# Retention and MLP on one core: order of the first loads, w_in's second half in two transfers, the last product in two PSUM banks

## Chip, core and metric

The kernel runs on one core of a Trainium2 chip. Its time is the device time of one launch, in microseconds. The core's engines are called PE (matmul), DVE (vector), ACT (scalar), POOL (GpSimd) and SP (sync); each runs its own instructions in order, and they wait for one another through semaphores. SP and ACT issue DMAs whose descriptors are made in hardware (queues q1 and q10 of the profile). POOL issues DMAs whose descriptors it makes itself (q0), and these can change the data type on the way. All three kinds run on the same 16 DMA engines.

## What is computed

```python
# q, k, v: [8, 8, 576, 64] float32; moe_w_in: [512, 2048]; moe_w_out: [2048, 512]
scores = (1 / sqrt(64)) * q @ k.transpose(0, 1, 3, 2)
gamma  = 1 - 2.0 ** (-5 - arange(8))
Dmat   = where(i >= j, gamma[h] ** (i - j), 0)
attn   = (scores * Dmat) @ v                     # [8, 8, 576, 64]
x      = attn.transpose(0, 2, 1, 3).reshape(4608, 512)
h      = x @ moe_w_in
out    = maximum(0.01 * h, h) @ moe_w_out        # [4608, 512] float32
```

The first part is a retention: attention without a softmax, with a decay per head. The second is an MLP with a leaky ReLU.

## The kernel before

**Units and groups.** The 4608 tokens are cut into 36 units of 128 tokens, two chunks of 64 each. A unit's q, k and v are 256 KB each (128 partitions x 512 float32), loaded by `load(u)` into tiles `t32` in the order k, q, v (x = 1, 0, 2). Four units make a group of 512 tokens, for which the MLP runs with float16 weights.

**Retention of a unit.** `cast_k` (ACT), `cast_q` and `cast_v` (DVE for the first eight units, POOL later) make float16 tiles, the last two with a decay multiplied in. The casted q and k are transposed, by PE into PSUM and a copy for units 0 to 7 (`transpose_pe`, `transposed`, `turn`), by a DMA that SP issues for the others (`transpose_dma`). `scores(u)` multiplies k with q inside a chunk and k with v for the state. `masks(u)` applies the causal mask on DVE. `state(u, j)` adds up the state on DVE, `state_cast` casts it. `outputs` or `outputs_acc` make the unit's 128 columns of x, which go to `xT`. `ahead(u)` is casts and transpose of a unit by ACT, POOL and SP.

**MLP.** `h_block`, `h_half` and `h_unit` are products with w_in (PE, L373), each followed by a leaky ReLU on ACT (L387) that empties an accumulator `acc`, of which there are four, one PSUM bank each. `h_half(g, a, fb)` takes half a of the group's tokens and 256 columns of the hidden layer, so fb = 0, 1 lie in the first quarter of w_in, fb = 2, 3 in the second, 4, 5 in the third and 6, 7 in the fourth. `halves` is several of these in a row. Group 0's product with w_out is `wide` (L423). Those of the other groups are `seven` (L483): seven products of 16 matmuls each in place of eight, with sums of weights (`w_mix`) and of activations (`mix`, DVE) prepared, and `keep` and `give` to bring the products p1, p5, p6 and p7 together. `give` writes a part of the output tile `osb`, and SP stores it. In the last group the second token half is stored in pieces: `give(1, 1, ...)` stores one, and the very last `give(1, 0, ...)` is done in two parts of 128 tokens.

**Order.** The program's order is written out by hand (`manual_schedule`), so the calls' order is each engine's order. It opens with `keep_warm` matmuls on zeros, the loads of units 0 to 7 with the weights between them, and the retention of units 0 to 3. Then groups 0 and 1 of the MLP are woven with units 4 to 7, and from there on each group's MLP is woven with the retention of later units.

**Loads at the start.** SP issues unit 0's k, the first half of its q and unit 1's k. ACT issues identity, constants and the other half of unit 0's q. POOL issues all the rest, in this order: v of unit 0, q and v of unit 1, units 2 and 3, the first two quarters of w_in, unit 4, the third quarter, unit 5, the fourth quarter, units 6 and 7, w_out. A quarter of w_in is two DMAs (64 partitions, four rows of 512 columns each, cast from float32 to float16). Each DMA of POOL uses one of eight semaphores in turn, and waits for the landing of the one eight before it. `behind` makes a DMA wait for other DMAs. `load(8)`, which SP issues, waits in this way for the third of the w_out loads.

Of the kernel before, what the change touches and what calls it, by code (L numbers as in the profile page):

```python
# [9 lines left out]
FP = mybir.dt.float32  # L10
F16 = mybir.dt.float16
MUL = mybir.AluOpType.mult
ADD = mybir.AluOpType.add
# [5 lines left out]
def kernel(  # L19
# [9 lines left out]
    nc = tc.nc  # L29
# [3 lines left out]
    P = 128  # L33
# [8 lines left out]
    HF, HN, HT = NF // 2, DM // 2, TOK // 2  # L42
# [99 lines left out]

    FQ = DFF // 4

    def load_w_in(f, after=None):
        fs = slice(f * FQ, (f + 1) * FQ)
        rows = moe_w_in.rearrange("(o c k) f -> o k c f", o=2, k=CH)
        ds = []
        for o in range(2):
            ds.append(nc.gpsimd.dma_start(out=w_in16[half(o), :, fs], in_=rows[o][:, :, fs]))  # L150
            if after is not None and not o:
                behind(ds[0], *after)
        return ds
# [298 lines left out]
    def g_part(g, a, b):  # L452
        return g_t[g][:, b * HF : (b + 1) * HF, a * HT : (a + 1) * HT]
# [15 lines left out]
    def seven(g, hooks, last=False):  # L469
# [2 lines left out]
        s = sums[g]  # L472

        def product(name, lhs, rhs, fresh):
            if fresh:
                r[name] = acc_pool.tile([P, 2, HN], FP, name="acc")
            order = (
                [(f, tb) for tb in range(2) for f in range(HF)]
                if last
                else [(f, tb) for f in range(HF) for tb in range(2)]  # L480
            )
            for n, (f, tb) in enumerate(order):
                nc.tensor.matmul(  # L483
                    out=r[name][:, tb, :],
                    lhsT=lhs[:, f, tb * P : (tb + 1) * P],
                    rhs=rhs[:, f, :],
                    start=fresh and n == 0,
                    stop=f == HF - 1,
                    skip_group_check=True,
                )  # L490

        def keep(name, of, plus=None):
            r[name] = m_pool.tile([P, 2, HN], FP, name=name)
            if plus is None:
                nc.scalar.copy(out=r[name], in_=r[of])
            else:
                nc.vector.tensor_tensor(out=r[name], in0=r[of], in1=r[plus], op=ADD)

        def give(a, b, of, plus=None, parts=1):
            if ("o", a) not in r:  # L500
                r["o", a] = o_pool.tile([P, 2, DM], FP, name="osb")
            for n in range(parts):
                ts = slice(n * 2 // parts, (n + 1) * 2 // parts)
                to = r["o", a][:, ts, b * HN : (b + 1) * HN]
                if plus is None:
                    nc.scalar.copy(out=to, in_=r[of][:, ts])
                else:
                    nc.vector.tensor_tensor(  # L508
                        out=to, in0=r[of][:, ts], in1=r[plus][:, ts], op=ADD
                    )  # L510
# [16 lines left out]
            ("p5", s[:, 0], w_mix[:, 0], True, lambda: keep("v", "p5", "u2")),  # L527
            ("p7", g_part(g, 1, 0), w_mix[:, 2], True, lambda: give(1, 1, "p7", "v")),
            ("p5", g_part(g, 0, 0), w_part(1, 1), False, lambda: give(0, 1, "p5", "u2")),
            (  # L530
                "p7", g_part(g, 1, 1), w_mix[:, 3], False,
                lambda: give(1, 0, "p7", "u2", 2 if last else 1),
            ),
        )
        if last:
            plan = (plan[0], plan[2], plan[1]) + plan[3:]
# [21 lines left out]
    pool_copy, act_copy, dve_copy = nc.gpsimd.tensor_copy, nc.scalar.copy, nc.vector.tensor_copy  # L558

    keep_warm(7)  # L560
    load(0, {1: nc.sync, 0: (nc.sync, nc.scalar), 2: nc.gpsimd})
    load(1, {1: nc.sync, 0: nc.gpsimd, 2: nc.gpsimd})
    load(2, nc.gpsimd)
    load(3, nc.gpsimd)
    load_w_in(0)
    load_w_in(1)
    load(4, nc.gpsimd)
    load_w_in(2)
    load(5, nc.gpsimd)
    load_w_in(3)  # L570
    load(6, nc.gpsimd)
    load(7, nc.gpsimd)
    w_out_loads = [d for n in range(4) for d in load_w_out(n)]


# [10 lines left out]
    for u in range(4):  # L586
# [7 lines left out]
        if not u:  # L594
            cast_q(1, nc.vector)
            cast_v(1, nc.vector)
        state(u, 1)
        if n < 4:
            transpose_pe(n, 1)
# [9 lines left out]
        if n < 3:  # L609
            cast_k(n + 1)  # L610
            cast_q(n + 1, nc.vector)
            cast_v(n + 1, nc.vector)
        if u < 3:
            state_cast(u, act_copy, (1,))
        if u == 1:
# [8 lines left out]
    def halves(g, *items):  # L624
        for a, fb in items:
            h_half(g, a, fb)
# [64 lines left out]
    halves(0, (0, 0), (0, 1))  # L691
    finish2(3)
    state_cast(3, act_copy, (1,))
    halves(0, (0, 2), (0, 3), (1, 0))
    cast_k(4)
    cast_qv(4)
    halves(0, (1, 1))
    turn(4, 1)
    halves(0, (1, 2))
    turn(4, 0)  # L700
# [128 lines left out]
```

## Time and profile before

| | |
|---|---|
| median of 14 runs | 292.47 us (291.36 to 297.07) |
| profiled execution | 291.36 us |
| its span, first to last instruction | 289.6 us |
| instructions | 9449 |
| busy PE, DVE, ACT, POOL | 281.1, 170.2, 144.2, 104.6 us |
| granted PE clock | 0.998 |
| read from HBM, written to it | 36.81 MB, 9.44 MB |
| first product with w_in begins | 18.66 us |

A line of the profile names engine and program line, then what an instruction writes and reads: "PE L373 MATMUL acc<-xT,w_in" is a product of line 373. A bracket at its end gives the idle time before it and who ended it. PEld is the weight load of a matmul. Stretches are given in microseconds from the start of the span. A row of a DMA view gives KB of one transfer and the median time from issue to landing; a row of a queue gives packets, megabytes and share of the 16 engines' time in that window. Busy POOL time in the first 36 us is mostly the issuing of DMAs.

### The profile page before, as it was taken

Reading aid. Unit: us, or ns where it says so; the run is one execution under the profiler, and the core shown is the slowest. Engines: PE = TensorE matmul, PEld = TensorE weight load, DVE = VectorE, ACT = ScalarE, POOL = GpSimd, SP = SyncE. Lnnn points to the kernel's source line nnn. Section 1 sums busy time; section 2 is a strip of 40 time slices with the busy share of each in tenths; the row PEclk is TensorE's granted clock in tenths of the full one; section 3 lists DMA queues with packets and bytes.
Section 4 is the critical chain, followed back from the end, with each engine's and each line's share of the span. In section 5 each row is a group of like instructions: output and inputs, shape, how many; then the busy total and the mean of one; then the engine's idle time right before and its main releaser. Section 6 shows DMA issues by size and latency. Waiting matters only on the chain.

```text
span 289.6 us, 9449 instructions
## 1 busy us (share of the span) xinstructions
PE 281.1 (97%) x4118; PEld 191.9 (66%) x4118; DVE 170.2 (59%) x293; ACT 144.2 (50%) x254; POOL 104.6 (36%) x124
## 2 busy tenths in 40 slices
PE   6999999999999999999999999999999999999994
PEld 2568888745874587458745874587458844874583
DVE  1875677964763595359635863586268636841342
ACT  3666766624327732773277327731773176317510
POOL 8959502843433324322524332234225413000000
PEclk9999999999999999999999999999999999999999
DMA  7999999998999977966896669788976151012003
GB/s 207 301 234 198 295 207 216 210 231 188 255 201 285 224 167 165 273 147 149 165 268 153 147 147 284 153 145 150 278 162 145 44 177 38 5 67 80 0 2 145
DMA packets 131738, 50.01 MB, mean 173 GB/s; under 512 B 121264, under 2 KB 126000, under 8 KB 131696
## 3 DMA queue, kind: packets, MB, share of 16 engines
q1 hardware_dynamic: 124864, 39.46, 58.7%
q0 software_dynamic: 6016, 9.70, 14.8%
q8 instruction: 32, 0.52, 0.7%
q10 hardware_dynamic: 816, 0.24, 0.3%
q14 instruction: 10, 0.08, 0.1%
HBM read 36.81 MB, written 9.44 MB: 160 GB/s over the span
## 4 chain that ended last, share of the span: by engine, by line
PE 91%; DVE 4%; DMA 2%; issue 1%; ACT 1%; ACTq 0%; DVEq 0%
PE acc L373 43%; PE acc L483 34%; PE acc L423 5%; PE sc L215 3%; DMA t<-in_q_dram 2%; PE ot L291 1%; PE sc L224 1%; PE ot L302 1%; PE ot L321 1%; PE acc L200 1%; DVE s L233 1%; DVE qk L175 1%; DVE v L179 1%; PE ot L333 0%; PE acc L551 0%
## 5 line engine op out<-in xcount | busy, mean ns | idle before, releaser
L373 PE MATMUL acc<-xT,w_in 128*128 128x512 f16 (+2 forms) x768 | 130.9, 326 | 0.0
L387 ACT ACTIVATE gt<-acc 128x512 f16<-128x512 f32 x144 | 85.9, 597 | 57.1 <-PE acc L373 55.4
L373 PEld LDWEIGHTS <-w_in 128*128 128x128 f16 x768 | 68.1, 98 | 51.3
L483 PEld LDWEIGHTS <-gt 128*128 128x128 f16 x640 | 61.8, 98 | 9.1
L233 DVE TENSOR_TENSOR s<-sc,cs 128x512 f16<-128x512 f32 x36 | 24.7, 687 | 40.8 <-PE sc L224 40.8
L273 POOL CAST st<-s 128x512 f16<-128x512 f32 x21 | 12.8, 610 | 93.5 <-DVE s L257 57.9
L483 PE MATMUL acc<-w_out,gt 128*128 128x256 f16 x384 | 45.9, 273 | 0.2
L355 ACT COPY own<-ot 128x512 f32<-128x512 f32 x30 | 17.6, 586 | 42.7 <-PE ot L302 34.9
L175 POOL TENSOR_TENSOR qk<-t,cs 128x512 f16<-128x512 f32 x28 | 30.6, 1094 | 15.6 <-DMA t<-in_q_dram 14.4
L179 POOL TENSOR_TENSOR v<-t,cs 128x512 f16<-128x512 f32 x28 | 31.6, 1130 | 0.2 <-PE acc L373 0.2
L467 DVE TENSOR_TENSOR mix<-gt 128x1024 f16<-128x1024 f16 x16 | 14.7, 916 | 29.0 <-ACT gt L387 29.0
L483 PE MATMUL acc<-w_mix,gt 128*128 128x256 f16 x256 | 30.6, 273 | 0.0
L483 PE MATMUL acc<-w_mix,mix 128*128 128x256 f16 x256 | 29.5, 273 | 0.0
L483 PEld LDWEIGHTS <-mix 128*128 128x128 f16 x256 | 25.0, 98 | 3.1 <-DVE mix L467 0.2
L172 ACT CAST qk<-t 128x512 f16<-128x512 f32 x36 | 22.3, 620 | 0.8 <-DMA t<-in_k_dram 0.6
L360 DVE TENSOR_TENSOR xT<-ot,own 128x512 f16<-128x512 f32 x30 | 20.5, 683 | 3.0 <-ACT own L355 3.0
L257 DVE TENSOR_TENSOR s<-sc,s 128x256 f32<-128x256 f32 x40 | 16.8, 420 | 3.3 <-PE sc L224 2.8
L508 DVE TENSOR_TENSOR osb<-acc,u 128x512 f32<-128x512 f32 (+1 forms) x17 | 11.1, 656 | 8.0 <-PE acc L483 8.0
L215 PEld LDWEIGHTS <-qkT 64*64 64x64 f16 x576 | 7.7, 107 | 11.2 <-issue 10.1
L276 POOL CAST st<-s 128x256 f16<-128x256 f32 x7 | 3.2, 454 | 32.2 <-DVE s L261 20.3
L423 PE MATMUL acc<-w_out,gt 128*128 128x512 f16 x64 | 14.3, 379 | 0.0
L467 DVE TENSOR_TENSOR mix<-mix,gt 128x1024 f16<-128x1024 f16 x16 | 14.0, 879 | 0.5
(52 smaller groups left out, 239.3 us busy)
## 6 DMA issues: line engine op xcount, KB each, us to landing
out_dram<-osb SPq DMA_DIRECT2D x17, 512.0 KB, 3.8
t<-in_k_dram SPq DMA_DIRECT2D x27, 256.0 KB, 3.9
t<-in_q_dram SPq DMA_DIRECT2D x25, 256.0 KB, 4.5
t<-in_v_dram SPq DMA_DIRECT2D x25, 256.0 KB, 4.9
w_in<-in_moe_w_in_dram POOLq DMA_DIRECT2D x8, 256.0 KB, 7.1
w_out<-in_moe_w_out_dram POOLq DMA_DIRECT2D x4, 512.0 KB, 9.9
t<-in_v_dram POOLq DMA_DIRECT2D x7, 256.0 KB, 5.3
t<-in_q_dram POOLq DMA_DIRECT2D x6, 256.0 KB, 5.7
```

What stands on the lines that cost most here:

```text
L172: nc.scalar.copy(out=qk16[u][:, 1], in_=t32[u, 1])
L175: eng.tensor_tensor(out=qk16[u][:, 0], in0=t32[u, 0], in1=decay(u, 0), op=MUL)
L179: eng.tensor_tensor(out=v16[u], in0=t32[u, 2], in1=decay(u, 1), op=MUL)
L233: nc.vector.tensor_tensor(out=s16s[u], in0=sc_tiles[u][:, :, 0], in1=mask_sb.unsqueeze(1).unsqueeze(1).to_broadcast([P, 2, NP, CH]), op=MUL,)
L257: nc.vector.tensor_tensor(out=to, in0=st, in1=carry[0], op=ADD)
L355: nc.scalar.copy(out=owns[u], in_=ot_tiles[u][:, :, 0:NP].rearrange("q j c t -> q c j t"))
L360: nc.vector.tensor_tensor(out=x_of(u).rearrange("q (c g) t -> q c g t", g=2), in0=ot_tiles[u][:, :, NP : 2 * NP].rearrange("q g (c j) t -> ...
L373: nc.tensor.matmul(out=hps[:, n, :], lhsT=w_in16[:, c, f * P : (f + 1) * P], rhs=xT[g][:, c, ts], start=(c == 0), stop=(c == NP - 1),)
L387: nc.scalar.activation(out=out, in_=in_, func=mybir.ActivationFunctionType.Lrelu)
L423: nc.tensor.matmul(out=ys[tb], lhsT=g_t[0][:, f, tb * P : (tb + 1) * P], rhs=w_out16[:, f, :], start=(f == 0), stop=(f == NF - 1),)
L467: nc.vector.tensor_tensor(out=z[:, fs], in0=a[:, fs], in1=b[:, fs], op=op)
L483: nc.tensor.matmul(out=r[name][:, tb, :], lhsT=lhs[:, f, tb * P : (tb + 1) * P], rhs=rhs[:, f, :], start=fresh and n == 0, stop=f == HF - ...
```

## The change

- Unit 0's v is issued in two halves by SP and ACT, behind their halves of q, in place of POOL.
- POOL's first DMA is then unit 1's q, and it waits for unit 0's k to land.
- `cast_v` of units 2 and 3 moves from behind `cast_q` to behind the mask of the unit before.
- The third and fourth quarter of w_in are loaded together, in two DMAs with rows of 1024 columns; the loads of units 5, 6 and 7 follow.
- In group 0, `h_half` (1, 0) moves behind the casts of unit 4.
- Casts and transpose of unit 9 (`ahead(9)`) come in front of `load(11)`.
- In the last group, p7 uses an accumulator for each of its two token blocks, with both of its `give` calls in two parts and stores.

```diff
-    def load_w_in(f, after=None):
-        fs = slice(f * FQ, (f + 1) * FQ)
+    def load_w_in(f, n=1, after=None):
+        fs = slice(f * FQ, (f + n) * FQ)
...
         def product(name, lhs, rhs, fresh):
+            apart = last and name == "p7"
             if fresh:
-                r[name] = acc_pool.tile([P, 2, HN], FP, name="acc")
+                r[name] = [
+                    acc_pool.tile([P, 1 if apart else 2, HN], FP, name="acc")
+                    for _ in range(2 if apart else 1)
+                ]
...
-                    out=r[name][:, tb, :],
+                    out=r[name][tb][:, 0, :] if apart else r[name][0][:, tb, :],
...
-                    start=fresh and n == 0,
+                    start=fresh and (f == 0 if apart else n == 0),
...
-        def give(a, b, of, plus=None, parts=1):
+        def give(a, b, of, plus=None):
+            parts = len(r[of])
...
-            (
-                "p7", g_part(g, 1, 1), w_mix[:, 3], False,
-                lambda: give(1, 0, "p7", "u2", 2 if last else 1),
-            ),
+            ("p7", g_part(g, 1, 1), w_mix[:, 3], False, lambda: give(1, 0, "p7", "u2")),
...
-    load(0, {1: nc.sync, 0: (nc.sync, nc.scalar), 2: nc.gpsimd})
-    load(1, {1: nc.sync, 0: nc.gpsimd, 2: nc.gpsimd})
+    load(0, {1: nc.sync, 0: (nc.sync, nc.scalar), 2: (nc.sync, nc.scalar)})
+    load(1, {1: nc.sync, 0: nc.gpsimd, 2: nc.gpsimd}, {0: (last_load[0, 1],)})
     load(2, nc.gpsimd)
     load(3, nc.gpsimd)
     load_w_in(0)
     load_w_in(1)
     load(4, nc.gpsimd)
-    load_w_in(2)
-    load(5, nc.gpsimd)
-    load_w_in(3)
-    load(6, nc.gpsimd)
-    load(7, nc.gpsimd)
+    load_w_in(2, 2)
+    for u in range(5, 8):
+        load(u, nc.gpsimd)
...
         if not u:
             cast_q(1, nc.vector)
             cast_v(1, nc.vector)
+        elif n < 4:
+            cast_v(n, nc.vector)
         state(u, 1)
...
             cast_q(n + 1, nc.vector)
-            cast_v(n + 1, nc.vector)
...
-    halves(0, (0, 2), (0, 3), (1, 0))
+    halves(0, (0, 2), (0, 3))
     cast_k(4)
     cast_qv(4)
-    halves(0, (1, 1))
+    halves(0, (1, 0), (1, 1))
...
+    ahead(9)
     load(11)
-    ahead(9)
```

More of the change, by code (lines that the diff above doesn't have):

```diff
@@ L494, in keep @@
             if plus is None:
-                nc.scalar.copy(out=r[name], in_=r[of])
+                nc.scalar.copy(out=r[name], in_=r[of][0])
             else:
-                nc.vector.tensor_tensor(out=r[name], in0=r[of], in1=r[plus], op=ADD)
-        def give(a, b, of, plus=None, parts=1):
+                nc.vector.tensor_tensor(out=r[name], in0=r[of][0], in1=r[plus], op=ADD)
+        def give(a, b, of, plus=None):
+            parts = len(r[of])
             if ("o", a) not in r:
@@ L505, in give @@
                 if plus is None:
-                    nc.scalar.copy(out=to, in_=r[of][:, ts])
+                    nc.scalar.copy(out=to, in_=r[of][n])
                 else:
                     nc.vector.tensor_tensor(
-                        out=to, in0=r[of][:, ts], in1=r[plus][:, ts], op=ADD
+                        out=to, in0=r[of][n], in1=r[plus][:, ts], op=ADD
                     )
```

## The prediction

> **What bounds the kernel now.** I read the busy line first, then the windows by stage, then the chain of waits.
>
> ```profile
> PE 281.1 (97%) x4118; PEld 191.9 (66%) x4118; DVE 170.2 (59%) x293; ACT 144.2 (50%) x254; POOL 104.6 (36%) x124
> ```
> ```profile
> 0.00:18.65 18.65, 15.07 (x278) 8.02 (x278) 10.70 (x24) 10.46 (x20) 15.28 (x24) 1.00 1.00 253
> 18.65:60.00 41.35, 40.71 (x704) 33.54 (x694) 29.92 (x51) 27.87 (x52) 21.42 (x23) 1.00 1.06 227
> 110.00:276.00 166.00, 165.84 (x2313) 108.81 (x2313) 95.59 (x160) 84.48 (x146) 48.56 (x56) 1.00 0.62 145
> ```
>
> The columns are the stretch, its length, busy time of PE, PEld, DVE, ACT and POOL, granted clock, DMA share, GB/s. From 18.65 us, when the first w_in product starts, PE has no room: 40.71 of 41.35 us, then 165.84 of 166. So the end moves only with the 18.65 us of start-up, with a hole made or filled behind it, and with what follows the last matmul. In start-up and up to 60 us the DMA engines are full (1.00 and 1.06).
>
> ```profile
> 1.70 4.48 DMA t<-in_q_dram
> ...
> 6.31 0.70 DVE qk L175
> ...
> 8.13 0.32 PE sc L215 x16
> ...
> 18.73 1.85 PE acc L373 x16
> ...
> 24.21 0.62 ACT qk L172
> ```
>
> This is the chain of waits (start, length, what). It begins with the half of unit 0's q that ACT issues. From 6.31 to 18.7 us it is arithmetic on DVE, PE and ACT, with no DMA in it.
>
> **Unit 0's loads and the gate.** The issue rows (KB, us to landing) and the DMA queues in 2.2 to 4.4 and in 4.4 to 6.6 us (packets, MB, share):
>
> ```profile
> t<-in_q_dram SPq DMA_DIRECT2D x1, 128.0 KB, 3.4
> t<-in_q_dram ACTq DMA_DIRECT2D x1, 128.0 KB, 4.5
> ```
> ```profile
> q1 hardware_dynamic: 1504, 0.38, 75.9%
> q10 hardware_dynamic: 513, 0.17, 30.9%
> q0 software_dynamic: 9, 0.04, 11.2%
> ```
> ```profile
> q0 software_dynamic: 117, 0.41, 52.4%
> q1 hardware_dynamic: 820, 0.21, 41.9%
> q10 hardware_dynamic: 159, 0.04, 7.9%
> ```
>
> Two equal halves of q: SP's lands at 1.25 + 3.4 = 4.65 us, ACT's at 6.2. Between the two, GpSimd's v of unit 0 arrives, in packets of 0.41 MB / 117 = 3.5 KB against 256 B on q1 and q10. The Trainium skill ("DMA: Bandwidth & Descriptors", Issuing engines are not separate DMA queues) speaks against this edit: issuing from several engines saves only issue time. By it the start moves by 0. The rows say that the kind of queue matters, since an equal half took 1.1 us longer beside q0. I take the rows: without q0's packets both halves end near 4.9 us (2.2 to 4.4 moved 2,017 hardware packets, 920 per us; ident, cs, k and q are about 2,300 from 2.0 us on). The q cast goes from 6.31 to about 5.0. v's 1,024 packets follow: landing about 5.9, in time for its cast at 6.0. Then transposes, ACT copy (0.58) and the idle matmuls in the old order: scores at 7.0 instead of 8.13.
>
> The issues added are one on SP (0.50) in front of unit 1's k and one on ACT (0.52), over at 2.8, a microsecond before ACT's first cast at 3.79. Unit 1's k is now behind v's half on SP: its packets end near 6.4, and GpSimd's may catch its tail. It lands at 7.3 to 8.0 (7.8 before); the transposes of that k need it by 7.3 to keep the whole 1.1 us. I take 0.9 us at the first w_in product (bounds 0.4 and 1.2): 17.75 us.
>
> The gate costs on POOL. Queued behind it are q and v of unit 1, units 2 to 7, all of w_in and w_out. k lands at 3.76, so q of unit 1 goes from 2.34 to about 3.85: all issues 1.5 us later. What of this reaches the landings lies between 0 (the DMA engines stay full with the same bytes, unit 0's v and unit 1's k filling the gap) and 1.5 (POOL's pace, 0.88 us for 256 KB, sets it); I take 0.5 to 0.9, since a load lands 4.7 to 5.0 us after its issue now, which holds some backlog. The first w_in quarter (9.95 + 6.9 = 16.8 for its second half) moves to 17.2 to 17.7: just in time. v of units 2 and 3 would be too late for DVE's old order; their casts move behind the mask, which covers it. That puts the state sum and its ACT cast 0.68 us later, in front of copies that had 0.58 idle: 0 to 0.15 us. Two casts of 0.68 stay two casts.
>
> **ACT order at unit 4.** The chain stops at ACT's k cast (24.21), behind one leaky more than it must be; PE waits 0.3 for it ("PE acc L200 <- ACT qk L172: 0.3"). With the (1, 0) block behind the casts this is gone if unit 4's k is there: it lands at 20.2 + 0.5 and is wanted at 22. Minus 0.3 us.
>
> **w_in's second half.** Four DMAs of 512 KB read become two of 1 MB, with unit 5's loads behind both.
>
> ```profile
> 18.29 0.63 POOL L150 DMA_DIRECT2D w_in<-in_moe_w_in_dram  x1 [0.52 <-DMA w_in<-in_moe_w_in_dram]
> 19.60 0.62 POOL L150 DMA_DIRECT2D w_in<-in_moe_w_in_dram  x1 [0.68 <-DMA w_in<-in_moe_w_in_dram]
> ```
> ```profile
> w_in<-in_moe_w_in_dram POOLq DMA_DIRECT2D x1, 256.0 KB, 6.1
> ```
> ```profile
> 27.55 1.92 PE L373 MATMUL acc<-xT,w_in 128*128 128x256 f16 x16
> ```
> ```profile
> 12.50:17.50 5.00, 4.41 (x108) 1.00 1.23 205
> ```
>
> In order: POOL's issues of the third quarter, the second one's time to landing (25.7 us), its first use on PE (27.55), and the rate while only w_in flows (205 GB/s of f16 written, so 410 read). There are 1.9 us of slack now. After the change the same use, columns 1024 on, needs both long DMAs, with the fourth quarter in them: 1 MB of f16 at 205 GB/s is 5.1 us. The page's ceiling (section Bandwidth: 435 GB/s) would make it 4.8; so long rows can give 0.3 us at most, and I take 5.1, the row. They follow unit 4's v, whose last part is issued at 17.09 and lands at 21.55; with the stream's 0.5 that is about 22.1, and both are in at about 27.2. PE gets there at 27.55 - 0.9 - 0.3 = 26.35. **It waits 0.85 us, and the start's gain shrinks to 0.35.** Bounds: 26.4 (DMA engines that skip the thin stretch at 20 to 24 us, where the share was 0.89) to 29.9 (see the rivals). Unit 5 is behind it: k at 28.0, v at 29.5, wanted from 30.4. Fewer issues (two of 0.65 us saved on POOL) are worth nothing, as POOL waits there for landings.
>
> **SP's swap.** The transpose of unit 9 passes load(11), three issues of 1.9 us together; these go from 55.50 to about 57.7. Unit 11's casts come at 65.9, scores of unit 9 at 64.28 wait for nothing: 0. The 8 us between hide it; without them ACT's cast would hold up the leaky blocks behind it by up to 2.2.
>
> **Last product.**
>
> ```profile
> 285.71 0.42 DVE osb L508
> 286.14 0.33 DVEq L824
> ```
>
> The last matmul ends at 285.69. Both 0.42 us additions wait for it, since they read one bank; the second ends at 286.47, its store is issued at 286.60, lands 1.77 later, and the closing takes 1.2. With two banks the first addition runs beside PE's last eight matmuls and only one is left: minus 0.42, bounds 0.2 (the 512 KB store of 284.72 still fills the DMAs until about 287) and 0.5. Paid for by one DVE addition (2 x 0.42 for 0.69) and one SP issue (0.37) more at 281 to 283, where DVE idles 1.05 us before each addition. The fifth accumulator reuses the buffer that ACT empties at 279.3; it is needed at 281.2. Nothing; without those 1.9 us PE would wait for the copy, 0.58 at most.
>
> **Sum.** At the third quarter's first use 0.35, rounded down to 0.25 for the casts' 0 to 0.15; tail 0.4: 0.65 us. Profiled execution 291.36 (span 289.6 and 1.76 around it) gives 290.7; the median, 1.11 above that execution, 292.47 - 0.65 = 291.8.
>
> **Rivals.**
> 1. No stall on w_in. The thin stretch at 20 to 24 us came from a queue one DMA deep; two 1 MB transfers fill it. If they land by 26.4, all is kept: 0.9 to 1.2 + 0.3 + 0.4 = 1.6 to 1.9, so 290.7. Against it: the last of unit 4's v already lands at 21.6, and 4.8 us is the best for what follows.
> 2. Slower: the long pair is late. The second DMA of the third quarter landed at 25.7 although 1.28 us of data stood behind 22.8: 1.6 us were lost in that stretch, and each of the 32 instruction fetches (q8, 0.7% of 16 engines' span) takes one DMA engine for 0.007 x 16 x 289.6 / 32 = 1.0 us. If both fall on the engine that is last, 27.2 + 1.6 + 1.1 = 29.9: the first use comes 2.35 later than before, less 0.4 at the end: 294.4. From a landing at 27.95 the kernel is slower, from 29.4 by over 0.5%. Only fewer dry stretches speak against it.
> 3. The edit does not do what it says: GpSimd's packets meet unit 1's k instead of unit 0's q, k lands at 8.3, and the start keeps its time. PE then reaches the use at 27.25 after a w_in that is there: 0.3 + 0.4, 291.8 too; with the later stream against it, 292.3.
>
> **Numbers.** Forecast 0.50, rival 1 0.23, rival 2 0.19, rival 3 0.08. 0.5% is 1.46 us, about what a measurement of this kernel can tell from no change. Faster by more: 0.20 of rival 1 and 0.04 of the forecast's good end, 0.24. Slower by more: 0.17 of rival 2. Within: 0.59. The forecast's own range is 291.1 to 292.9; with rival 1 down to 290.3 and the near part of rival 2 up to 293.9.
>
> **What would show it.** Right: unit 0's q cast near 5.0 us, scores(0) near 7.0, the first w_in product near 17.8, no wait before the transposes of unit 4's k, a PE gap ended by the w_in DMA near 26.4 to 27.2, one DVE addition after the last matmul, and PE dense between. Wrong: q still landing after 6 us; unit 1's k landing after 8; a gap on w_in at the first block (17 to 18 us) instead; a second store that lands 1.7 us after the last matmul in spite of the earlier addition; any DMA wait on PE, DVE or ACT behind 30 us.

## Result and the profile after

| | before | after |
|---|---|---|
| median | 292.52 us (291.33 to 297.07) | 296.18 us (294.61 to 296.76) |
| profiled execution, its span | 291.36, 289.6 us | 296.37, 294.6 us |
| granted PE clock, mean | 0.998 | 0.994 |
| busy PE | 281.1 us | 282.7 us |

The ratio of times, after to before, is 1.0112 (1.0081 to 1.0143). This and every later ratio is taken over undisturbed runs of both kernels on one chip. The change makes the kernel slower by 1.1%, about 3.3 us; I had predicted 0.7 us less than before.

The busy line of the page and the group of the w_in product (instructions, busy us, mean ns, then idle time before them and who ended it):

```profile
PE 282.7 (96%) x4118; PEld 192.8 (65%) x4118; DVE 169.9 (58%) x294; ACT 144.3 (49%) x254; POOL 101.7 (35%) x121
```
```profile
L373 PE MATMUL acc<-xT,w_in 128*128 128x512 f16 (+2 forms) x768 | 132.2, 328 | 4.4 <-DMA w_in<-in_moe_w_in_dram 4.4
```

The same 4118 matmuls take 1.6 us more PE time, and the w_in product waits 4.4 us for its weights. The windows by stage say where:

```profile
0.00:18.65 18.65, 15.18 (x278) 8.03 (x278) 10.95 (x25) 10.61 (x20) 12.70 (x20) 1.00 0.90 209
18.65:60.00 41.35, 36.72 (x636) 31.67 (x637) 25.38 (x46) 24.84 (x47) 20.31 (x23) 0.96 1.02 222
110.00:276.00 166.00, 165.84 (x2326) 109.97 (x2325) 97.57 (x164) 82.09 (x142) 51.18 (x59) 1.00 0.66 150
```

The last row is the dense one of before, busy 165.84 of 166 us. In the middle row PE is busy 36.72 us of 41.35, where it had been 40.71, and the clock is 0.96. In the first row the DMA engines, full before (1.00, 253 GB/s), are at 0.90 and 209 GB/s.

The chain of waits, from its start (start, length, what):

```profile
0.73 3.06 DMA t<-in_k_dram
3.80 0.30 issue
4.10 7.24 POOL t L132 x8
11.34 1.85 POOL w_in L150 x3
13.18 9.35 DMA w_in<-in_moe_w_in_dram
...
22.81 8.52 DMA w_in<-in_moe_w_in_dram
31.33 0.14 issue
31.46 2.92 PE acc L373 x16
```

Before, the chain began with ACT's half of q and was arithmetic from 6.31 us on. Now it begins with the gate: unit 0's k lands, POOL issues its first DMA at 4.10, then eight loads and w_in one behind the other, a w_in DMA lands and releases the second DMA of the long pair, and that lands at 31.33. Down to there not one step is arithmetic.

PE's waits up to 60 us (us in total, times, longest) and three rows of its timeline:

```profile
PE acc L373 <- DMA w_in<-in_moe_w_in_dram: 4.4, 3, 2.6
```
```profile
20.03 1.91 PE L373 MATMUL acc<-xT,w_in 128*128 128x256 f16 x16 [1.52 <-DMA w_in<-in_moe_w_in_dram]
...
31.46 2.92 PE L373 MATMUL acc<-xT,w_in 128*128 128x256 f16 x16 [2.58 <-DMA w_in<-in_moe_w_in_dram]
...
34.89 2.25 PE L373 MATMUL acc<-xT,w_in 128*128 128x256 f16 x16
```

The first product with w_in begins at 20.03 us, 1.37 later than before; the first use of the third quarter at 31.46, 3.91 later. Those 16 matmuls then take 2.92 us instead of 1.92, and 16 more take 2.25 at 34.89. The clock row by row (length, PE busy, clock, DMA share, GB/s) gives the reason:

```profile
31.00:32.00 1.00, 0.54 (x5) 1.00 1.01 336
32.00:33.00 1.00, 1.00 (x8) 0.59 1.02 340
33.00:34.00 1.00, 1.00 (x7) 0.50 1.03 344
34.00:35.00 1.00, 1.00 (x35) 0.50 1.07 356
35.00:36.00 1.00, 1.00 (x8) 0.71 1.00 317
```

From 32.18 us on the clock is at half for 3.4 us. By the end of that stretch the loss has grown from 3.91 to 5.43 us (37.19 against 31.76 for the same instruction), and it stays: the last matmul ends at 291.15 instead of 285.69, 5.46 later. The tail gives back 0.46.

### The profile page after: what moved, and what is told of

Its sections match the earlier page's. It is cut to its first block, busy times and chain, and to the rows that moved or that the text cites. A ratio compares the mean times of both kernels' runs of the same rounds, so it can differ in the third digit from the quotient of the medians.

```text
span 294.6 us, 9452 instructions
## 1 busy us (share of the span) xinstructions
PE 282.7 (96%) x4118; PEld 192.8 (65%) x4118; DVE 169.9 (58%) x294; ACT 144.3 (49%) x254; POOL 101.7 (35%) x121
## 4 chain that ended last, share of the span: by engine, by line
PE 86%; DMA 7%; POOL 3%; DVE 2%; issue 1%
PE acc L373 40%; PE acc L487 33%; DMA w_in<-in_moe_w_in_dram 6%; PE acc L423 5%; POOL t L132 2%; PE sc L215 2%; PE ot L291 1%; PE ot L302 1%; PE sc L224 1%; DMA t<-in_k_dram 1%; POOL w_in L150 1%; PE ot L321 1%; DVE s L233 0%; PE acc L200 0%; DVE s L261 0%
## 5 line engine op out<-in xcount | busy, mean ns | idle before, releaser
L175 POOL TENSOR_TENSOR qk<-t,cs 128x512 f16<-128x512 f32 x28 | 30.4, 1086 | 15.5 <-DMA t<-in_q_dram 14.1
L179 POOL TENSOR_TENSOR v<-t,cs 128x512 f16<-128x512 f32 x28 | 31.0, 1109 | 1.6 <-DMA t<-in_v_dram 1.6
L467 DVE TENSOR_TENSOR mix<-gt 128x1024 f16<-128x1024 f16 x16 | 14.0, 878 | 28.8 <-ACT gt L387 28.8
L467 DVE TENSOR_TENSOR mix<-mix,gt 128x1024 f16<-128x1024 f16 x16 | 13.1, 826 | 0.5
```

Source lines behind the costliest of these rows:

```text
L175: eng.tensor_tensor(out=qk16[u][:, 0], in0=t32[u, 0], in1=decay(u, 0), op=MUL)
L467: nc.vector.tensor_tensor(out=z[:, fs], in0=a[:, fs], in1=b[:, fs], op=op)
```

## The experiments

| kernel | profiled us | median (lowest to highest) | ratio to before (95%) |
|---|---|---|---|
| a1_tail: before, two banks at the end | 293.75 | 292.78 (291.16–296.44) | 0.998 (0.9951–1.0008) |
| a2_win: before, long pair | 295.11 | 293.64 (291.37–296.69) | 1.001 (0.9979–1.0041) |
| a3_start: before, new start | 294.02 | 294.13 (293.13–296.33) | 1.0055 (1.0026–1.0085) |
| a4_nogate: after, no gate | 301.56 | 300.29 (292.44–301.71) | none |
| b1_nowin: after, old w_in order | 292.79 | 292.83 (292.02–295.18) | 1.001 (0.9984–1.0035) |
| b2_short: after, pair in short rows | 293.8 | 293.74 (292.29–295.61) | 1.0007 (0.9985–1.0029) |
| b3_small: before, the rest of the change | 291.3 | 291.36 (290.17–296.42) | 0.9953 (0.9925–0.9981) |
| c1_warm: after, PE kept busy | 295.34 | 294.99 (294.15–296.71) | 1.0064 (1.0041–1.0087) |
| c2_poolq: before, all of q on POOL | 291.78 | 293.38 (291.78–295.51) | 1.0003 (0.9979–1.0027) |
| d1_gate: before, gate alone | 293.89 | 294.24 (292.77–295.86) | 1.004 (1.0016–1.0065) |
| e3_spq: before, all of q on SP | 291.04 | 291.28 (290.66–291.97) | 0.9947 (0.9927–0.9966) |
| e4_best: e3_spq and b3_small | 290.71 | 290.19 (289.99–290.71) | 0.9898 (0.9868–0.9928) |
| f1_early: after, gate on the identity | 292.75 | 293.79 (291.59–296.39) | 1.0016 (0.9992–1.0040) |
| f2_pair: e4_best, long pair | 291.15 | 291.23 (290.59–294.45) | 0.9954 (0.9929–0.9979) |

### The parts by themselves: a1_tail, a2_win, a3_start, b3_small

a1_tail is before with only the two-bank last product, a2_win with only the long pair and its order, a3_start with only the two `load` lines and the moved v casts, b3_small with the two-bank product, the moved (1, 0) block and the swap of `ahead(9)` and `load(11)`.

```diff
 a3_start
-    load(0, {1: nc.sync, 0: (nc.sync, nc.scalar), 2: nc.gpsimd})
-    load(1, {1: nc.sync, 0: nc.gpsimd, 2: nc.gpsimd})
+    load(0, {1: nc.sync, 0: (nc.sync, nc.scalar), 2: (nc.sync, nc.scalar)})
+    load(1, {1: nc.sync, 0: nc.gpsimd, 2: nc.gpsimd}, {0: (last_load[0, 1],)})
 a2_win
-    load_w_in(2)
-    load(5, nc.gpsimd)
-    load_w_in(3)
...
+    load_w_in(2, 2)
```

a1_tail, expected:

> The kernel before with the two-bank last product alone. In the changed kernel one addition of 0.42 us stands behind the last matmul and the span ends 3.4 us after it, against 3.9 before. Every theory of the loss puts it in the first 40 us, so all expect minus 0.4 us here (ratio 0.9985). Should it come out slower, the extra accumulator is at fault.

a2_win, expected:

> The kernel before with w_in's third and fourth quarter as one long pair alone, no gate. Theory G (the gate starves POOL's stream, which then runs dry and late; the pair only shows it): the pair lands at 21.6 + 5.1 = 26.7 us, before PE wants it at 27.55, so the time stays within 0.3 us. Theory W (the pair itself is the cause, since the third quarter now waits for the fourth and long rows are no faster): PE waits 2.5 us or more at 27.55, and the time rises by 2.5 to 4 us.

a3_start, expected:

> The kernel before with unit 0's v on SP and ACT, the gate and the moved v casts alone; w_in in quarters as before. Theory G: the first quarter lands at 19 to 20 us as in the changed kernel, the first product begins 1.4 us late, the later quarters arrive just in time, and the time rises by 1.2 to 2.5 us. Theory W: the start gains what I predicted, 0.3 to 0.9 us.

b3_small, expected:

> The kernel before with the parts of the change that touch neither the first loads nor w_in: the last product in two banks, the (1, 0) block behind unit 4's casts, unit 9's casts and transpose in front of load(11). In the traces the first is worth 0.45 us behind the last matmul, the second 0.3 to 0.5 us at unit 4's transposes, the third nothing: minus 0.7 us, ratio 0.9975. If unit 4's casts hold up ACT instead, it stays at 0.9985.

Measured: the new start by itself costs 0.55%, about 1.6 us. The small parts together bring 0.47%, about 1.4 us (the interval is 0.6 to 2.2; 0.7 was expected); the tail alone (0.998, with 1 inside its interval) is too small to be shown by times. The long pair without the gate shows no difference, but its interval leaves room for 1.2 us, and f2_pair below does find a cost. Multiplied, 1.0055 x 1.001 x 0.9953 gives 1.002, and the change has 1.0112. Each factor is uncertain by 0.3%, so the 0.9%, 2.7 us, that is left over is more than the parts explain: most of it appears only when the new start and the long pair stand together.

Only a part of a3_start's loss is a wait for w_in. Its profiled execution is 2.7 us longer than that of before; PE waits 0.17 and 0.35 us for w_in, and 1.52 us much later:

```profile
67.03 0.32 PE L215 MATMUL sc<-qkT 64*64 64x64 f16 x16 [1.52 <-DMA qkT<-qk]
```

This is the transpose of unit 9. The gate makes the whole of POOL's queue late, w_out too, and `load(8)` waits for the third w_out load: SP issues it at 46.57 us (43.55 before). The transpose of unit 9 stands behind `load(11)` on SP; it is issued at 61.50 us (57.78 before) and lands at 66.98. In after, `ahead(9)` stands in front of `load(11)`, the transpose lands at 63.73, and PE does not wait for it. So the swap, which I had priced at nothing, seems to hide a part of the gate's cost in after; no run has after without it.

A lesson in reading lies in a1_tail. Its profiled execution is 2.4 us longer than that of before, though the edit touches nothing ahead of 280 us. Its waits on PE and its start-up window:

```profile
PE acc L200 <- DVE qk L175: 2.6, 1, 2.6
```
```profile
0.00:18.65 18.65, 14.02 (x206) 6.86 (x207) 9.05 (x21) 8.82 (x16) 15.60 (x24) 0.91 0.99 250
```

In this execution ACT's half of unit 0's q landed at 7.42 us (6.18 in that of before), PE waited 2.6 us for its cast, and the clock fell to half after it. a2_win has the same (7.64 us), so that PE came to the pair only at 31.26 and found it there, landed at 27.98: this profile does not show what the pair costs PE. Before's start varies by itself; e3_spq below shows a part of the reason.

### Is it the gate? d1_gate and a4_nogate

d1_gate puts the gate into before, with unit 0's v still POOL's first DMA; a4_nogate takes it out of after.

```diff
 d1_gate
-    load(1, {1: nc.sync, 0: nc.gpsimd, 2: nc.gpsimd})
+    load(1, {1: nc.sync, 0: nc.gpsimd, 2: nc.gpsimd}, {0: (last_load[0, 1],)})
 a4_nogate
-    load(1, {1: nc.sync, 0: nc.gpsimd, 2: nc.gpsimd}, {0: (last_load[0, 1],)})
+    load(1, {1: nc.sync, 0: nc.gpsimd, 2: nc.gpsimd})
```

d1_gate, expected:

> The kernel before with the gate alone: unit 0's v is still POOL's first DMA at 1.3 us, unit 1's q behind it waits for unit 0's k. Theory G (the gate's delay and the thin queue behind it make w_in late): POOL's q of unit 1 goes out near 4.0, w_in's first quarter lands at 18.5 or later, the first product starts 0.5 to 1.5 us late, and the time rises by 0.5 to 1.5 us. If v's move to SP and ACT makes the stream late and not the gate: no more than 0.3 us.

a4_nogate, expected:

> The changed kernel without the wait of POOL's first DMA for unit 0's k; all else as changed. Theory G: POOL's issues start at 1.3 us again, w_in's first quarter lands near 16.8, the pair near 26.5 to 27.5, and the time is within 0.7 us of the kernel before, that is 3 us or more below the changed one. Theory W: the pair is as late as in the changed kernel and the time stays 2.5 us or more above the kernel before.

d1_gate costs 0.4%, most of a3_start's 0.55%, and its w_in quarter is in at 19.26 (16.81 before, 19.04 in a3_start, 19.89 after). The gate shows in its timeline of POOL, and the first product with w_in in that of PE:

```profile
4.18 0.89 POOL L132 DMA_DIRECT2D t<-in_q_dram  x1 [1.82 <-DMA t<-in_k_dram]
```
```profile
19.63 1.92 PE L373 MATMUL acc<-xT,w_in 128*128 128x256 f16 x16
```

The product is 0.97 us late, as theory G foretold, but not for G's reason: w_in is there, and no wait stands in front of it. In this execution ACT's half of q landed at 6.78 us (6.18 before), and PE waited 1.82 us for its cast (1.28 before). What the profile does show of the gate is a wait of 0.71 us for the transpose of unit 9, as in a3_start. That late w_in loads cost PE time is shown by after, b1_nowin and f1_early, not by this profile.

a4_nogate was a miss for both theories. Without the gate the median is 300.29 us, above either kernel; one of the six runs took 292.44 us, the others 297.2 to 301.7 (too far apart for a ratio). The profile is of one of the others. Its waits on PE and its first window:

```profile
PE acc L200 <- DVE qk L175: 3.1, 1, 3.1
PE ot L321 <- DVE s L233: 3.0, 3, 2.0
PE acc L200 <- ACT qk L172: 2.2, 1, 2.2
```
```profile
0.00:18.65 18.65, 11.97 (x93) 5.08 (x94) 5.19 (x12) 5.07 (x8) 14.62 (x23) 0.73 1.01 250
```

POOL's packets here meet every load of the hardware queues: ACT's half of q lands at 7.83 us, the halves of v at 8.04 and 8.49, and unit 1's k, issued by SP at 2.41, only at 14.09. The DMA engines are as full as before (1.01 and 250 GB/s), with the wrong bytes first. PE idles 8.3 us in these waits, 6.3 of them in the first 26 us, and the clock's mean in the first window is 0.73. So the gate does protect units 0 and 1; once v hangs on SP and ACT, leaving the gate out was worse than having it in five of six runs. What is too dear is its length, and what it holds back.

### How long a gate? f1_early

```diff
-    nc.scalar.dma_start(out=ident, in_=i_dram.ap())
+    ident_load = nc.scalar.dma_start(out=ident, in_=i_dram.ap())
...
-    load(1, {...}, {0: (last_load[0, 1],)})
+    load(1, {...}, {0: (ident_load,)})
```

> The changed kernel with POOL's first DMA waiting for the identity's landing (2.4 to 2.9 us) in place of unit 0's k (3.8): POOL starts near 3.1 instead of 4.1. If lateness follows the gate in proportion, w_in's first quarter and the pair land 1 us earlier, PE's wait at the pair goes from 2.6 to 1.6, too short for the clock to fall: the time drops by 1.0 to 2.4 us. If the missing backlog is the larger part, they land 1.5 us or more earlier and the time drops by 2.5 us. If POOL's packets now catch unit 0's v and unit 1's k on the hardware queues instead, k of unit 1 lands after 8.5 and the time does not drop at all.

The identity lands about a microsecond before k, and POOL's first DMA goes out at 3.09 instead of 4.10. The first w_in quarter is in at 17.66, the pair at 29.23 (2.1 us sooner than after). In the six profiles with the long gate (after, a3_start, b1_nowin, b2_short, c1_warm, d1_gate) the first quarter is in at 19.04 to 19.89, so one microsecond of gate buys 1.4 to 2.2 of landing. The first use of the third quarter:

```profile
29.37 1.91 PE L373 MATMUL acc<-xT,w_in 128*128 128x256 f16 x16 [1.49 <-DMA w_in<-in_moe_w_in_dram]
```

1.49 us of wait, the clock stays up, and 1.0016 in place of 1.0112. Unit 1's k lands at 7.72, as ever: this gate is long enough. Where the second microsecond comes from is read in the window from 7 to 10 us, in which all three kernels move nothing but units' loads (columns: length, POOL busy, PE clock, DMA share, GB/s). Before, after, f1_early:

```profile
7.00:10.00 3.00, 3.00 (x5) 1.00 1.04 344
```
```profile
7.00:10.00 3.00, 3.00 (x4) 1.00 0.95 269
```
```profile
7.00:10.00 3.00, 3.00 (x4) 1.00 1.03 333
```

After the long gate the DMA engines carry 75 GB/s less for three microseconds, 0.22 MB, which is 0.65 us at the rate of before. The six profiles with the long gate have 262 to 293 GB/s here, the nine without a gate 317 to 346. POOL goes on issuing one 256 KB load each 0.88 us, 298 GB/s. I read the lower rate as the missing backlog: when no loads stand issued and waiting, nothing lets the DMA engines run above POOL's pace. The shorter gate gives the rate back, which fits. But the rate of after lies below even that pace, and no run changed the backlog alone.

Load by load the lateness against before grows: unit 1's q lands 0.6 us later, unit 2's q 1.2, unit 3's q 2.6, the first w_in quarter 3.1. POOL's issues of the last three are each 2.0 us late. So at first the backlog does hide the gate; by unit 3 it no longer does. A second thin stretch lies from 13 to 16 us. Before and after:

```profile
13.00:16.00 3.00, 2.76 (x76) 1.64 (x74) 2.93 (x7) 2.48 (x5) 2.30 (x4) 1.00 1.23 203
```
```profile
13.00:16.00 3.00, 2.80 (x78) 1.79 (x77) 2.97 (x7) 2.26 (x6) 2.91 (x5) 1.00 0.78 131
```

The share is 0.76 to 0.97 in the six profiles with the long gate, and 1.20 to 1.24 without one, except for c2_poolq's 0.97. In after an instruction fetch takes one DMA engine for 0.96 us from 12.75 us on, just ahead of this stretch; in before one begins at 14.48, while the queue is full. Whether such a stop costs more when little is queued was not tested. A gate of 1.76 us (2.34 to 4.10) plus 0.2 us (its first DMA now takes 1.08 us, which v bore before) makes 1.96 us of issue; the rest of the 3.1 us by which w_in is late lies between issue and landing (8.0 us from issue to landing for that DMA, 6.9 before). Why the time to landing grows was not isolated.

### What the pair adds: b1_nowin, b2_short, f2_pair

b1_nowin has w_in's quarters in the old order, b2_short the new order in short rows, and f2_pair the pair in e4_best, where there is no gate.

```diff
 b2_short
-    load_w_in(2, 2)
+    load_w_in(2)
+    load_w_in(3)
```

b1_nowin, expected:

> The changed kernel with w_in's third and fourth quarter and unit 5 to 7 in the old order of POOL's queue; everything else as changed. If the pair costs its 2.6 us wait and 1.3 us of half clock only because the gate makes the stream late, both go here: 3 to 4 us below the changed kernel, and no better than 0.3% above to 0.2% below the kernel before, since the gate's own 1.2 to 1.6 us stay and the tail and unit 4's casts give back 0.7. If the gate is harmless and the pair was everything, it is 0.3% or more below the kernel before.

b2_short, expected:

> The changed kernel with the third and fourth quarter in four DMAs with rows of 512 columns, in the same place of POOL's order. If long rows are slow in themselves, PE's wait of 2.6 us at the third quarter is gone and the time falls by 1.5 us or more. If what counts is the lateness of the stream, four DMAs carry the same bytes, but the third quarter need not wait for the fourth: its second DMA lands 2.5 us before the pair's, PE's wait goes from 2.6 to below 0.5, and the time falls by 2.5 to 3.5 us. If neither, it stays within 0.3 us of the changed kernel.

f2_pair, expected:

> The kernel before with q on SP and the three small parts (e4_best) and, added to it, w_in's second half as one long pair; no gate. In e4_best PE first uses the third quarter at 27.0 us, and v of unit 4 lands at 21.0. The pair needs 4.8 to 5.1 us from there: 25.9 to 26.3, so it is in time and the time equals e4_best's within 0.3 us, if the pair only hurts behind a late stream. If it hurts in itself it lands at 27.5 to 28.5 as in a2_win, and the time rises by 0.5 to 1.5 us over e4_best.

The first use of the third quarter in the timelines of b1_nowin, b2_short and f2_pair:

```profile
28.52 1.91 PE L373 MATMUL acc<-xT,w_in 128*128 128x256 f16 x16 [0.15 <-DMA w_in<-in_moe_w_in_dram]
```
```profile
30.18 1.91 PE L373 MATMUL acc<-xT,w_in 128*128 128x256 f16 x16 [1.34 <-DMA w_in<-in_moe_w_in_dram]
```
```profile
27.51 1.91 PE L373 MATMUL acc<-xT,w_in 128*128 128x256 f16 x16 [0.56 <-DMA w_in<-in_moe_w_in_dram]
```

b1_nowin: with the gate and without the pair the kernel is even with before (1.001), as a3_start and b3_small multiplied (1.0008) say. The wait is 0.15 us, and the change loses its 1% to the pair on top of the gate, the half clock included.

b2_short splits this. In short rows the third quarter is in at 30.04 and the fourth at 32.76; in long rows both are in at 31.33. Long rows do bring the same bytes in sooner, by 1.4 us in after and by 1.0 in c1_warm (31.76). But the third quarter is wanted first, and in long rows no column of it is complete before the last of the fourth. PE waits 1.34 us instead of 2.58 (below 0.5 was expected: the third quarter is 1.3 us ahead of the pair, not 2.5), its clock stays up, and the time is that of b1_nowin.

f2_pair is what I had priced, the pair without the gate. It was to land at 25.9 to 26.3 and in time; it lands at 27.38, and PE waits 0.56 us. Its cost against e4_best is 0.4 us by the profiled executions and 1.6 us by the two ratios, which come from two chips. So the pair costs a little by itself, and more behind the gate. From the last landing of unit 4's v to its own it takes 6.05 us here (from 21.33), 6.04 in a2_win (21.94 to 27.98) and 6.52 in after (24.81 to 31.33), where my sum had 5.1. The window of after up to its landing:

```profile
24.80:31.30 6.50, 4.08 (x70) 3.45 (x68) 2.60 (x6) 3.20 (x6) 4.80 (x6) 1.00 1.07 235
```

The DMA engines are full and move 1.53 MB, of which the pair is at most 1.05. I read the rest as the loads behind it: unit 5's k is issued at 23.42 and lands at 31.72, 0.4 us after the pair. My sum had given the engines to the pair alone.

### What the clock adds: c1_warm

```diff
+    keep_warm(10)
     halves(0, (0, 4), (0, 5))
```

> The changed kernel with ten matmuls on zeros in front of the first use of the third quarter, so that PE is busy while it waits for the pair. Nothing arrives earlier. In the changed kernel the 16 matmuls behind the wait took 2.92 us where the kernel before has 1.92, and the granted clock of 18.65 to 60 us was 0.96. Theory C (the idle time costs a second time, through the clock): that block takes 1.9 us again and the time falls by 1.0 to 1.6 us. Without such an effect the time stays or rises by up to 0.5 us.

Ten matmuls on zeros fill part of the wait, and nothing else changes. The timeline's row and the window:

```profile
31.90 1.91 PE L373 MATMUL acc<-xT,w_in 128*128 128x256 f16 x16 [1.05 <-DMA w_in<-in_moe_w_in_dram]
```
```profile
18.65:60.00 41.35, 38.99 (x685) 32.86 (x686) 26.56 (x47) 26.31 (x50) 20.34 (x22) 1.00 1.04 224
```

The pair is even later here (31.76), the use begins 0.44 us later than after, and the kernel is still faster: 1.0064 against 1.0112, 0.48% or 1.4 us. The 16 matmuls take 1.91 us instead of 2.92, and the window's clock is 1.00 instead of 0.96. So the half-clock spell alone costs about 1.4 us of the 3.3, as the timeline of after says (1.00 + 0.33 us in its two rows). Each ratio is uncertain by 0.2 to 0.3%; but the one run of after with a mean clock of 1.000 took 294.61 us, 1.6 under the median, which agrees.

How long must PE wait for this? In the traces the granted clock changes only in steps of 3.41 us. In after, the step from 28.76 to 32.18 us holds the whole wait of 2.58 us, and the next step is at half clock. Two waits at the start narrow it down. Each lies in one step; the rows are that step and the next one. First d1_gate, where PE is idle for 1.82 us, then a2_win, where it is for 2.24 (length, then PE busy; the clock is the third number from the end):

```profile
5.08:8.49 3.41, 1.59 (x11) 0.58 (x9) 1.29 (x2) 0.98 (x2) 3.41 (x4) 1.00 1.02 277
8.49:11.91 3.42, 3.05 (x68) 1.88 (x68) 2.64 (x5) 1.29 (x3) 3.42 (x6) 1.00 0.96 284
```
```profile
5.85:9.27 3.42, 1.18 (x9) 0.43 (x7) 1.29 (x2) 0.38 (x2) 3.42 (x5) 1.00 1.09 343
9.27:12.68 3.41, 3.41 (x43) 1.67 (x42) 2.29 (x5) 1.31 (x3) 3.40 (x7) 0.50 1.01 324
```

In all sixteen traces, a step at full clock with up to 1.82 us of idle PE time is followed by full clock, and one with 2.24 or more (a2_win, a1_tail, a4_nogate, after) by half clock.

### Who is late at the start: c2_poolq, e3_spq, e4_best

Both give unit 0's q one queue, and keep v on POOL without a gate. c2_poolq takes POOL's, in front of v, e3_spq SP's, behind k. e4_best is e3_spq with the parts of b3_small.

```diff
 c2_poolq
-    load(0, {1: nc.sync, 0: (nc.sync, nc.scalar), 2: nc.gpsimd})
+    load(0, {1: nc.sync, 0: nc.gpsimd, 2: nc.gpsimd})
 e3_spq
-    load(0, {1: nc.sync, 0: (nc.sync, nc.scalar), 2: nc.gpsimd})
+    load(0, {1: nc.sync, 0: nc.sync, 2: nc.gpsimd})
```

c2_poolq, expected:

> The kernel before with all of unit 0's q issued by POOL, as its first DMA, and no gate: only k of units 0 and 1 are left on SP. Theory S (hardware queues starve as soon as POOL's packets flow, so what is urgent must be in POOL's queue or be over before it): q of unit 0 lands at 5.2 to 5.6 us instead of 6.2 to 7.6, v at 6.2, k of unit 1 as before, the spread of the runs shrinks, and the median falls by 0.7 to 1.5 us. If POOL's first DMA is slow in itself, q lands at 6.3 as v did, and the time stays.

e3_spq, expected:

> The kernel before with all of unit 0's q on SP, right behind its k, in one DMA; POOL and its first load as before. Theory H (the half on ACT is late because it sits behind the 74 KB of constants and in a second hardware queue, and is then caught by POOL's packets at 4.1 us): on SP alone its 1,024 packets follow the k at about 1,000 per us and are over by 4.6 us; q lands at 4.8 to 5.4, the first product with w_in begins 0.5 to 1.0 us earlier, slow starts at half clock become rare, and the ratio is 0.995 to 0.998. If the descriptors' making is the limit and not the queue, q lands at 5.8 or later as in the changed kernel, and nothing changes.

e4_best, expected:

> The kernel before with q on SP and the three small parts together. By theory H and the traces the gains add up: 0.5 to 1.0 us at the start and 0.7 us behind it, ratio 0.993 to 0.996. If q on SP does nothing, it equals the three small parts alone.

c2_poolq missed: q lands at 6.08, no sooner than before, and the time is the same (1.0003). e3_spq hits. The issue row of q (KB, us to landing; issued at 1.25) and the first product:

```profile
t<-in_q_dram SPq DMA_DIRECT2D x1, 256.0 KB, 3.8
```
```profile
18.09 1.92 PE L373 MATMUL acc<-xT,w_in 128*128 128x256 f16 x16
```

All 256 KB on SP land at 5.05 us; half of it on ACT had needed until 6.18, with the same v on POOL beside it. The kernel gains 0.53%, and its times draw together, 290.66 to 291.97 us in place of before's 291.3 to 297.1. That is not ACT's half alone: c2_poolq and f2_pair have no half of q on ACT either, and their times spread by 3.7 and 3.9 us. With b3_small's parts, e4_best has 290.19 us, 1.0% under before and about 2.1% under after (0.9898 / 1.0112). It reaches the third quarter at

```profile
27.00 1.92 PE L373 MATMUL acc<-xT,w_in 128*128 128x256 f16 x16
```

with w_in already there.

## Why the prediction was wrong

**What bounds the kernel: right.** From the first w_in product on, PE has no room. All 5.4 us lost by 37 us are found again at the last matmul (5.46), and no DMA wait follows on PE behind 31.5 us.

**Unit 0's q: mechanism too simple, a small term.** I said that without POOL's packets both halves of q end near 4.9 us. The issue rows of after:

```profile
t<-in_q_dram SPq DMA_DIRECT2D x1, 128.0 KB, 3.2
```
```profile
t<-in_q_dram ACTq DMA_DIRECT2D x1, 128.0 KB, 4.1
```

The first goes out at 1.25 and lands at 4.5, the second at 1.70 and lands at 5.8, although POOL's first DMA is not issued before 4.10. Here the halves are 1.3 us apart, where before they were 1.5. In the six profiles of this start with a gate (after, a3_start, b1_nowin, b2_short, c1_warm, f1_early) they are 0.8 to 1.5 us apart, in the six with POOL's packets beside them (before, a1_tail, a2_win, b3_small, d1_gate, a4_nogate) 1.5 to 3.4. So ACT's half is late by itself, and POOL's packets make it later; I had put down the whole to the packets. The rows of POOL's gate and of the q cast:

```profile
4.10 1.08 POOL L132 DMA_DIRECT2D t<-in_q_dram  x1 [3.66 <-DMA t<-in_k_dram]
...
5.92 0.69 DVE L175 TENSOR_TENSOR qk<-t,cs 128x512 f16<-128x512 f32 x1 [4.64 <-DMA t<-in_q_dram]
```

The cast starts at 5.92 (6.31 before, 5.0 predicted), scores(0) at 7.74 (7.0 predicted), and PE is ready for w_in at 18.5, 0.15 us sooner than before instead of 0.9. In the five other profiles of this start PE is ready at 18.67 to 19.48 (before: 18.66), so a gain is not shown at all.

The rule of the Trainium skill that I weighed ("DMA: Bandwidth & Descriptors", Issuing engines are not separate DMA queues) was closer for this edit: by it the start moves by 0, by my rows 0.9, measured 0.15. Read as "the queue makes no difference" it does not hold here: moving half of q from ACT to SP (e3_spq) is worth 0.5%, and unit 1's k on SP lands at 7.6 us in after and at 14.1 in a4_nogate, where POOL's queue runs beside it from the start. Which queues carry the loads decides when one of them lands, though the bytes are the same.

**The gate's lateness in the stream: the step that failed.** I wrote that of 1.5 us "what of this reaches the landings lies between 0 ... and 1.5", and took 0.5 to 0.9. The issue is 1.96 us late and the landing of the first w_in quarter 3.1 us (19.89 against 16.81), outside the bounds at the far end. No profile with the long gate has it before 19.04, and none of those without a gate after 17.18, but for c2_poolq (17.87), which has a load more in front of it. I took the 4.7 to 5.0 us between issue and landing as a backlog that hides a later issue for good. It does so for the first loads (0.5 to 0.6 us late, as I said), but the gate uses it up, and from then on the lateness grows beyond that of the issue. The shorter gate of f1_early gives back 1.4 to 2.2 us of landing for 1.0 of gate. That the gate is the cause is shown by this; that it acts through the backlog is my reading. "Just in time" (17.2 to 17.7) became a wait of 1.52 us and one of 0.35.

**Order of unit 4: right.** No wait on ACT is left before its k's transposes. The matmuls at 25.11 before are at 26.38, 1.27 later, where the two w_in waits less the start's 0.15 make 1.72: about 0.45 us gained, for 0.3 predicted.

**The pair: right place, its start and its own time too small.** That the start's gain would be lost at the third quarter's first use, because that use needs both DMAs, is what the timeline shows. That f2_pair lands at 27.38, so near my 27.2, is luck: it has no gate and starts from 21.33, not 22.1, and then takes 6.05 us instead of 5.1. After the gate both DMAs are issued at 21.46 and 22.81 and land at 28.39 and 31.33. Its row of the second one, and of the wait in front of its issue:

```profile
w_in<-in_moe_w_in_dram POOLq DMA_DIRECT2D x1, 512.0 KB, 8.5
```
```profile
22.81 0.62 POOL L150 DMA_DIRECT2D w_in<-in_moe_w_in_dram  x1 [0.72 <-DMA w_in<-in_moe_w_in_dram]
```

The landing is 4.1 us behind the forecast. 2.7 of these are the stream's lateness, with which the pair starts (unit 4's v in at 24.81 instead of 22.1). The other 1.4 are the pair's own time, 6.52 instead of 5.1: I took the rate of a stretch in which only w_in flows, and unit 5's loads flow beside the pair.

**The clock: missing from the sum.** No step priced a slower clock, and none of the rivals did. It cost 1.4 us (c1_warm). The rule stands in the Trainium skill ("TensorE: Matmul & The Clock Gate", Part 1: The HAM clock gate: half clock after an idle window of about 3.4 us, whose phase is its own). The traces agree on the 3.41 us and on the free phase (steps begin at 4.87 us in after, at 5.85 in a2_win). But by the page's letter a wait of 2.58 us is short enough; the trace shows that it was not, nor was 2.24 us in a2_win, while 1.49 us (f1_early) and 1.82 us (d1_gate) left the clock up.

**SP's swap and the casts: no cost seen, and a gain that I missed.** Behind a late stream the transpose of unit 9 has a price without the swap: PE waits 1.52 us for it in a3_start and 0.71 in d1_gate, and not at all in after. PE is dense from 60 us on, and the DVE waits for v at the start come to 0.5 us, off the chain.

**Tail: right.** The two last additions of after, and the end of the chain:

```profile
290.30 0.42 DVE L513 TENSOR_TENSOR osb<-acc,u 128x256 f32<-128x256 f32 x1 [0.18 <-PE acc L487]
291.17 0.43 DVE L513 TENSOR_TENSOR osb<-acc,u 128x256 f32<-128x256 f32 x1 [0.45 <-PE acc L487]
```

The first runs while PE works in the other bank; only one follows the last matmul, which ended at 291.15. 3.4 us from there to the end, 3.9 before: minus 0.46 for minus 0.42. That is the rule of the Trainium skill too ("PSUM — Partial Sum Buffer", Summary: rules for kernel authors: read one bank while the matmul runs in another).

**The rivals.** Rival 2, the late pair, is what happened, and more: it put the landing at 29.9 and the time at 294.4. Its cause was another in the main, though. I built it from instruction fetches and dry stretches (and added 1.1 us for fetches that I had reckoned at 1.0); the gate that I had in my own list supplies 2.7 us of delay, as much as both together. A fetch and a thin stretch do stand in the trace of after, at 12.75 and from 13 to 16 us, and what they add to the gate's delay was not separated. Rival 1 (no stall) failed with the pair's landing, rival 3 with unit 1's k, which landed at 7.62.

**The sum again,** in the profiled execution: first use of the third quarter 3.91 later instead of 0.25 sooner, 4.16 us of the error; half clock 1.33; rest until the last matmul 0.22; tail 0.06 better (0.46 for 0.40). That is 5.65, and 290.7 + 5.65 = 296.35, where 296.37 was measured.

## What to carry to other kernels

A gate in front of a queue that feeds everything later can cost more than its own length (here 1.96 us of issue became 3.1 us of landing); so gate on the earliest landing that does the job, and follow the delay to the last load of that queue before pricing anything else. Two transfers joined in one are as late as the later of them: join them only where both are wanted at one time, or where the trace shows that much slack after every other part of the change. And price a PE wait of two microseconds or more with the slower clock behind it (here 1.82 us was harmless and 2.24 was not), or fill it with idle matmuls.

## What the runs showed of the hardware

- Half the load on each of the two hardware queues does not land at one time. ACT's 128 KB half of q landed 0.8 to 1.5 us after SP's equal half without POOL's packets and 1.5 to 3.4 us after it with them, as late as 7.64 us in a2_win; the whole 256 KB on SP landed at 5.05. Before's times spread from 291.3 to 297.1 us, those of e3_spq, without ACT's half, by 1.3 us; a part of the scatter comes from there, but f2_pair, without it too, has 3.9. Why ACT's half is behind was not isolated.
- POOL's packets, 3.5 KB each in the queue rows of before against 256 B on the hardware queues, can stretch a 256 KB hardware load from about 5 to 11.7 us from issue to landing (unit 1's k in after and in a4_nogate).
- A PE wait of 2.24 us inside one 3.41 us step of the clock (a2_win) was enough for the next step to be at half clock, and 1.82 us (d1_gate) was not. In after the spell cost 1.4 us.
- Rows twice as long in DRAM brought the last of the same 2 MB read in 1.0 to 1.4 us sooner (31.76 and 31.33 against 32.76), more than the 0.3 us that I had allowed by estimate.
- A DMA queue that a gate made 2.0 us late landed its loads 0.6 us late at first and 3.1 us late eleven microseconds on.
